# Engines' programs in the main sequence instead of a block, in a decode kernel on one core

## Chip, cores and metric

The kernel runs on one core of one Trainium2 chip. The metric is the device time of one execution in microseconds (us); lower is better. The time before is the median of three runs, 193.99 us (193.94 to 194.02).

A core has five engines, each with an instruction stream of its own: TensorE (PE, its weight loads PEld), VectorE (DVE), ScalarE (ACT), GpSimd (POOL) and SyncE (SP). They meet only through semaphores. SP, ACT and POOL can issue DMAs, which 16 DMA engines carry out.

## What is computed

One token of a decoder layer: normalised input, grouped-query attention against a cache of 16384 keys and values (32 query heads, 8 key/value heads, head size 128), an output projection and a residual; then a second normalisation and an MLP. The reference, cut to what matters (the data are bfloat16):

```python
def _A_ref(x, k_cache, v_cache, wq, wo):       # x [1,1,512], caches [1,8,16384,128]
    q = (x @ wq).reshape(B, Sq, 32, 128).transpose(0, 2, 1, 3)
    k = jnp.repeat(k_cache, 4, axis=1)
    v = jnp.repeat(v_cache, 4, axis=1)
    p = softmax(einsum("bhqd,bhkd->bhqk", q, k) * 128 ** -0.5)
    o = einsum("bhqk,bhkd->bhqd", p, v)
    return o.transpose(0, 2, 1, 3).reshape(B, Sq, 4096) @ wo

def _B_ref(x, w1, w2, w3, w4):                 # with one token hs is zero: w1, w2 drop out
    ...
    x1 = x + hs
    h2 = gelu(layernorm(x1) @ w3) @ w4         # w3 [512,1792], w4 [1792,512]
    return x1 + h2

h  = A_x + _A_ref(layernorm(A_x), A_k_cache, A_v_cache, A_wq, A_wo)
h2 = h + _B_ref(layernorm(h), B_w1, B_w2, B_w3, B_w4)
```

With a single token the four shifted quarters of the mixer are all padding, so hs is zero and the kernel doesn't load w1 and w2.

## The kernel before

The 79 MB of keys, values and weights are streamed through four buffers `rb` of 4 MB (`RING`, line 124), in the order of `ORDER` (line 125): wq, the keys of two heads, then values and keys in turn, at last wo and the MLP's weights. All these loads are issued by SP through `load` (line 216); only the small input x4 is issued by ACT (line 302). The loop of line 444 runs over the 8 key/value heads: DVE transposes a head's keys in eight pieces (line 379), PE multiplies them by the queries (line 387), a maximum over all scores is taken (lines 394 to 408), ACT applies the exponential (line 409), and PE multiplies the weights by the values of the head before (line 428). Behind the loop stand the output projection (line 494), the normalisation, the two MLP products (lines 507 and 528) and the last addition, which writes the tile `fin` on DVE (line 532). SP stores `fin` (line 534), a DMA of 4 rows of 256 bytes, and a no-operation on SP that is marked as reading `out` (line 536) makes SP wait until the store has landed.

How the code becomes instruction streams is what matters here. The class `Program` (line 24) collects operations: `op` (line 35) appends each to the list of its engine, `self.ops`, and notes which earlier operations it depends on. Nothing is written until `emit` (line 72). It numbers the operations that someone waits for and gives each engine a semaphore that counts them (lines 77 to 85). Then it opens a block (line 86) and, for each engine, hands the function that `_engine` returns (line 92) to the block's method for this engine (lines 87 to 89); the function goes through the engine's list and writes each operation's waits (line 102) and the operation itself (line 104). The block is entered through the `ExitStack` that the kernel opens at line 150, so that it is left where that `with` ends. For this reason the profile puts the instructions of the block's end under L150: a branch, a drain on each engine (it waits until what the engine has in flight is done) and a meeting of all engines over two semaphores, which GpSimd gathers and releases.

A meeting of the same kind stands at the program's start, ahead of the kernel's own instructions. It is written where the program object is made, and the profile has it under L553, with four small constants that GpSimd fills.

Of the kernel before, what the change touches and what calls it, by code (L numbers as in the profile page):

```python
# [23 lines left out]
class Program:  # L24
# [47 lines left out]
    def emit(self):  # L72
        for ops in self.ops.values():
            for o in ops:
                for d in o.deps:
                    d.needed = True
        for e, ops in self.ops.items():
            if not any(o.needed and o.dma is None for o in ops):
                continue
            sem = self.ctx.enter_context(self.nc.semaphore(f"e_{e}"))  # L80
            n = 0
            for o in ops:
                if o.dma is None and o.needed:
                    n += 1
                    o.sem, o.val = sem, n
        block = self.ctx.enter_context(self.nc.Block())
        for e, at in (("SP", block.sync), ("POOL", block.gpsimd), ("PE", block.tensor),
                      ("ACT", block.scalar), ("DVE", block.vector)):
            at(self._engine(self.ops[e]))

    @staticmethod
    def _engine(ops):
# [475 lines left out]
```

## Time and profile before

| | us |
|---|---|
| median of three runs | 193.99 (193.94 to 194.02) |
| profiled execution, its time | 193.82 |
| its span, first to last instruction | 191.7 |
| PE busy | 118.5 (62%) |
| DVE busy | 107.6 (56%) |
| ACT busy | 10.0 (5%) |
| POOL busy | 8.8 (5%) |
| DMA queue of the loads, share of 16 engines | 96.9% |
| read from memory | 79.17 MB, 413 GB/s over the span |
| mean granted TensorE clock | 0.87 |

A profile is one execution. Its span goes from the first to the last recorded instruction; the execution's time is a little longer, as something is done ahead of and behind the recorded instructions. The page gives the busy time of each engine over the span; instructions that only the engine's sequencer handles (semaphore instructions, branches, drains, the issue of a DMA) are not counted as busy, and an engine's name with a q (SPq, ACTq) stands for its sequencer. The chain of waits is followed back from the last instruction: at each step to whatever released it.

The page's strip of the busy share in 40 equal slices, in tenths (9 is 90% or more), shows how steady the stream of loads is and how the last slice differs:

```profile
DMA  6999999999999999999999999999999999999991
```

### The profile page before, as it was taken

The page shows a single profiled execution, that of the slowest core. Times are in us where ns is not written, and L with a number is a line of the kernel's source. Part 1 is how long each engine was busy: PE and PEld are TensorE (multiplying, and loading weights), DVE is VectorE, ACT ScalarE, POOL GpSimd, SP SyncE. Part 2 cuts the span into 40 slices and gives each one's busy share as a digit, 9 for nine tenths or more (in the row PEclk, how much of TensorE's full clock was granted, in tenths as well). Part 3 has the DMA queues.
Part 4 walks back from the last instruction along what each step waited for, and adds up shares of the span by engine and source line. Part 5 has one row for each costly group of instructions (what it writes and reads, how often), then busy time and mean ns, then how long its engine had stood idle before and what let it go on. Part 6 is the DMA issues. An engine that isn't in the chain of part 4 may idle for free.

```text
span 191.7 us, 2236 instructions
## 1 busy us (share of the span) xinstructions
PE 118.5 (62%) x962; PEld 53.1 (28%) x962; DVE 107.6 (56%) x178; ACT 10.0 (5%) x22; POOL 8.8 (5%) x19
## 2 busy tenths in 40 slices
PE   1025079479799825982499349953994399456343
PEld 1024024124243321432143213331332133214211
DVE  5822099498589318932793269426952595203260
ACT  3000000100100100010001000010001000400010
POOL 6400000000000000000000000000000000000060
PEclk9999999969969985999589966997999579969955
DMA  6999999999999999999999999999999999999991
GB/s 219 438 438 434 438 439 431 438 438 438 431 427 438 438 438 424 427 397 424 424 431 438 434 438 438 438 431 438 431 431 421 438 431 438 391 412 404 424 378 49
DMA packets 3912, 79.29 MB, mean 414 GB/s; under 512 B 448, under 2 KB 448, under 8 KB 1216
## 3 DMA queue, kind: packets, MB, share of 16 engines
q1 hardware_dynamic: 3896, 79.17, 96.9%
q8 instruction: 7, 0.11, 0.2%
q14 instruction: 1, 0.01, 0.0%
q10 hardware_dynamic: 8, 0.00, 0.0%
HBM read 79.17 MB, written 0.00 MB: 413 GB/s over the span
## 4 chain that ended last, share of the span: by engine, by line
DMA 66%; DVE 21%; PE 5%; SPq 5%; issue 1%; ACT 0%; ACTq 0%
DMA rb<-in_A_k_cache_dram 56%; DVE kt L379 20%; DMA rb<-in_B_w_dram 10%; SPq L217 5%; PE s_ps L387 5%; ACT p_sb L409 0%; DVE pt L414 0%; DVE mx L394 0%; PE mn_ps L528 0%; PE mn_ps L404 0%; PE mn_ps L398 0%; DVE nm L400 0%; DVE fin L532 0%; DVE nmh L406 0%; SPq L102 0%
## 5 line engine op out<-in xcount | busy, mean ns | idle before, releaser
L387 PE MATMUL s_ps<-kt,qb 128*128 128x512 bf16 x256 | 71.9, 442 | 34.8 <-DVE kt L379 34.3
L379 DVE STREAM_TRANSPOSE kt<-rb 128x1024 int32<-128x1024 int32 x64 | 73.0, 1207 | 30.1 <-DMA rb<-in_A_k_cache_dram 30.1
L387 PEld LDWEIGHTS s_ps<-kt,qb 128*128 128x128 bf16 x256 | 26.2, 109 | 77.9 <-DVE kt L379 44.3
L428 PE MATMUL O_ps<-rb,pt 128*16 128x512 bf16 x256 | 20.3, 404 | 3.7 <-DMA rb<-in_A_v_cache_dram 3.7
L439 PE MATMUL A_ps<-o_sb,zo 128*128 128x128 f32 x64 | 9.7, 296 | 7.4 <-DVE o_sb L436 7.4
L409 ACT ACTIVATE p_sb<-s_ps,bias 128x512 bf16<-128x512 f32 x8 | 5.5, 687 | 154.8 <-DVE nmh L406 154.8
L394 DVE TENSOR_REDUCE mx<-s_ps 128x1 f32<-128x512 f32 x8 | 5.5, 692 | 10.0 <-PE s_ps L387 10.0
L439 PEld LDWEIGHTS A_ps<-o_sb,zo 128*128 128x128 f32 x64 | 8.1, 197 | 8.5 <-DVE o_sb L436 8.5
L436 DVE COPY o_sb<-O_ps 128x512 f32<-128x512 f32 x8 | 5.3, 657 | 8.1 <-PE O_ps L428 8.1
L414 DVE STREAM_TRANSPOSE pt<-p_sb 128x512 bf16<-128x512 bf16 x8 | 5.7, 712 | 7.2 <-ACT p_sb L409 7.2
L358 PE MATMUL mn_ps<-xn,rb 128*128 128x1 bf16 x128 | 3.6, 165 | 9.3 <-DMA rb<-in_A_wq_dram 9.3
L428 PEld LDWEIGHTS O_ps<-rb,pt 128*16 128x16 bf16 x256 | 5.8, 91 | 10.4 <-DMA rb<-in_A_v_cache_dram 5.6
L292 POOL TENSOR_SCALAR st<-st 128x1 f32<-128x1 f32 x1 | 0.3, 264 | 175.6 <-DVE st L277 175.6
L358 PEld LDWEIGHTS mn_ps<-xn,rb 128*128 128x128 bf16 x128 | 3.5, 104 | 9.3 <-issue 9.3
L398 PE MATMUL mn_ps<-ident_f,mx 128*1 128x128 f32 x16 | 3.0, 270 | 2.5 <-DVE mx L394 2.5
L418 PE MATMUL A_ps<-acc,zd 128*128 128x1 f32 x16 | 3.1, 260 | 2.3 <-ACT p_sb L409 2.3
L400 DVE TENSOR_REDUCE nm<-mn_ps 1x4 f32<-1x128 f32 x8 | 2.2, 279 | 3.8 <-PE mn_ps L398 3.8
L343 POOL MEMSET qb<- 128x4992 bf16 x1 | 4.3, 4257 | 0.0
L494 PE MATMUL O_ps<-rb,o_b 128*32 128x128 bf16 x128 | 2.3, 220 | 2.7 <-DMA rb<-in_A_wo_dram 1.6
L418 PEld LDWEIGHTS A_ps<-acc,zd 128*128 128x128 f32 x16 | 2.4, 188 | 5.9 <-ACT p_sb L409 5.9
L362 DVE CAST QT<-mn_ps 128x32 bf16<-128x32 f32 x1 | 0.2, 193 | 6.0 <-PE mn_ps L358 6.0
L528 PE MATMUL mn_ps<-rb,hcol 128*32 128x128 bf16 x56 | 2.3, 307 | 2.0 <-DVE hcol L523 1.2
(72 smaller groups left out, 42.4 us busy)
## 6 DMA issues: line engine op xcount, KB each, us to landing
rb<-in_A_k_cache_dram SPq DMA_DIRECT2D x8, 4096.0 KB, 29.7
rb<-in_A_v_cache_dram SPq DMA_DIRECT2D x8, 4096.0 KB, 35.0
rb<-in_A_wq_dram SPq DMA_DIRECT2D x1, 4096.0 KB, 12.2
rb<-in_A_wo_dram SPq DMA_DIRECT2D x2, 1280.0 KB, 30.1
rb<-in_B_w_dram SPq DMA_DIRECT2D x1, 1344.0 KB, 23.5
rb<-in_A_wo_dram SPq DMA_DIRECT2D x1, 1024.0 KB, 32.4
rb<-in_B_w_dram SPq DMA_DIRECT2D x1, 640.0 KB, 25.3
rb<-in_A_wo_dram SPq DMA_DIRECT2D x1, 512.0 KB, 33.2
```

Of the source, the lines that this page charges most:

```text
L217: P.op(by, lambda e: e.dma_start(dst, src), w=[key, *also], dma=name)
L343: pool(lambda e: e.memset(qb[:, :, :, :], 0.0), w=["qb"])
L358: pe(lambda e, h=h, k=k: e.matmul(n_ps[:, h:h + 1], wq_sb[:, k * HQ * DH + h * DH:k * HQ * DH + (h + 1) * DH], xn[:, k:k + 1], start=(k == ...
L379: dve(lambda e, i=i, view=view: e.transpose(view(kt), view(rb[i])), r=[("r", i, n) for n in range(RPARTS)], w=[("kt", t)])
L387: pe(lambda e, g=g, n=n, c=c: e.matmul(s_ps[:, g % 2, :], qb[:, n, g, QPAD - 4 * c:QW - 4 * c], ktv[:, n // 2, n % 2, :, 8 * c:8 * c + 8, ...
L394: dve(lambda e, g=g: e.tensor_reduce(mx[:, :], s_ps[:, g % 2, :], AX.X, ALU.max), r=[("s", g % 2)], w=["mx"], bank=[("s", g % 2)])
L409: act(lambda e, g=g: e.activation(p_sb[:, :], s_ps[:, g % 2, :], ACTF.Exp, bias=bias[:, 0:1], scale=float(SCALE), accum_out=acc[g % 2][:, :]),
L414: dve(lambda e, g=g: e.transpose(pt[g % 2][:, :, :].rearrange("p n u -> p (n u)"), p_sb[:, :]), r=["p"], w=[("pt", g % 2)])
L418: pe(lambda e, g=g: e.matmul(A_ps[:, 128:129], zd[:, 112 - 16 * g:240 - 16 * g], acc[g % 2][:, :], start=(g == 0), stop=(g == HKV - 1), sk ...
L428: pe(lambda e, q=q, ct=ct, xl=xl, ch=ch: e.matmul(O_ps[g % 2][32 * ct:32 * ct + 16, :], pt[g % 2][:, xl, 4 * ch:4 * ch + 16], tiles[:, xl ...
L436: dve(lambda e, g=g: e.tensor_copy(o_sb[g % 2][:, :], O_ps[g % 2][:, :]), r=[("O", g % 2)], w=[("osb", g % 2)], bank=[("O", g % 2)])
L439: pe(lambda e, g=g, j=j: e.matmul(A_ps[:, 0:128], zo[:, j, 112 - 16 * g:240 - 16 * g], o_sb[g % 2][:, j * 128:(j + 1) * 128], start=False, ...
```

## The change

`emit` no longer opens a block. It calls the function of each engine with the engine object itself, so that the operations are written into the sequence the program is in already, the main one, behind its opening meeting. The engines are gone through in a slightly different order (ACT second instead of fourth). Everything else is as it was: the lists of operations, their semaphores and waits, the store and the no-operation on SP behind it.

```diff
@@ -83,10 +83,9 @@
                 if o.dma is None and o.needed:
                     n += 1
                     o.sem, o.val = sem, n
-        block = self.ctx.enter_context(self.nc.Block())
-        for e, at in (("SP", block.sync), ("POOL", block.gpsimd), ("PE", block.tensor),
-                      ("ACT", block.scalar), ("DVE", block.vector)):
-            at(self._engine(self.ops[e]))
+        for e, eng in (("SP", self.nc.sync), ("ACT", self.nc.scalar), ("POOL", self.nc.gpsimd),
+                       ("PE", self.nc.tensor), ("DVE", self.nc.vector)):
+            self._engine(self.ops[e])(eng)
 
     @staticmethod
     def _engine(ops):
```

## The prediction

> **What bounds the kernel now.** I read the chain of waits first, because only work on it can move the end. By its shares the kernel is a stream of loads: DMA 66%, then the key transposes on VectorE. The change touches none of that. So the second view is the chain in order of time, its last pieces:
>
> ```profile
> 169.27 19.55 DMA rb<-in_B_w_dram
> 188.82 0.04 issue
> 188.86 0.43 PE mn_ps L528 x6
> 189.30 0.02 issue
> 189.32 0.29 DVE fin L532
> ```
>
> The columns are start, length and what it was, in us. The reader is to see that the last piece of arithmetic ends at 189.32 + 0.29 = 189.61, while the span is 191.7: two microseconds lie behind it, and the change is there. The third view, the timeline of the last stretch, names the next step:
>
> ```profile
> 189.64 0.63 SPq L534 DMA_DIRECT2D out_dram<-fin  x1
> ```
>
> SyncE issues the store of the result at 189.64 and has issued it at 190.27. The fourth view is SyncE's own waits:
>
> ```profile
> SPq L150 <- DMA out_dram<-fin: 1.0, 1, 1.0
> SPq L553 <- PEq L553: 0.7, 1, 0.7
> SPq L150 <- PEq L150: 0.2, 1, 0.2
> ```
>
> SyncE waits 1.0 us for the store to land, and then 0.2 us more for a meeting of the engines. L150 is the line under which the block's end is recorded, L553 the program's opening meeting. The view of line 150 is the thing removed, all of it (count, shortest/median/longest in ns, first and last start in us):
>
> ```profile
> L150 POOLq EVENT_SEMAPHORE  x2: 17/17/17, 191.5 to 191.6; - x2
> L150 ACTq DRAIN  x1: 879/879/879, 185.1 to 185.1; - x1
> L150 POOLq DRAIN  x1: 564/564/564, 186.4 to 186.4; - x1
> L150 PEldq DRAIN  x1: 450/450/450, 188.9 to 188.9; - x1
> L150 DVEq DRAIN  x1: 326/326/326, 189.3 to 189.3; - x1
> L150 SPq COMPARE_BRANCH  x1: 33/33/33, 191.3 to 191.3; - x1
> L150 SPq DRAIN  x1: 7/7/7, 191.4 to 191.4; - x1
> L150 SPq EVENT_SEMAPHORE  x1: 17/17/17, 191.6 to 191.6; - x1
> L150 ACTq EVENT_SEMAPHORE  x1: 17/17/17, 191.6 to 191.6; - x1
> L150 DVEq EVENT_SEMAPHORE  x1: 21/21/21, 191.6 to 191.6; - x1
> L150 PEldq EVENT_SEMAPHORE  x1: 51/51/51, 191.6 to 191.6; - x1
> ```
>
> Four engines have drained by 189.7; everything else of the meeting hangs on SyncE's branch, which carries the wait on the store. The view rounds starts to 0.1 us; the same records in nanoseconds, with the store's last increment ahead of them, are
>
> ```
> 191277         store's semaphore reaches its value
> 191293 .. 191326  SyncE  COMPARE_BRANCH
> 191449 .. 191456  SyncE  DRAIN
> 191482 .. 191499  GpSimd EVENT_SEMAPHORE (gather)
> 191559 .. 191576  GpSimd EVENT_SEMAPHORE (release)
> 191601 .. 191618  SyncE  EVENT_SEMAPHORE
> 191614 .. 191665  TensorE EVENT_SEMAPHORE, end of the span
> ```
>
> **The change part by part.** The profiled execution took 193.82 us and its span is 191.665, so 2.155 us lie around the span and no row shows them. The median of the runs shown is 193.99; I work out a difference on the profiled execution and take it off the median.
>
> Removed from the path: from the branch's start to the last release, 191.665 - 191.293 = 0.372 us. It is made of the branch (0.033), what lies between a taken branch and the next instruction (0.123), SyncE's drain (0.007), the step to GpSimd (0.026), its two semaphore instructions and the gap between them (0.094), the step to TensorE (0.038) and TensorE's semaphore instruction (0.051).
>
> Left in its place: SyncE still waits on the store, now on the no-operation of L536 or on a semaphore instruction, with nothing behind it. The trace of before has neither at this place: the wait had moved onto the branch. The nearest rows are SyncE's semaphore instruction, 0.017, and the branch without its jump, 0.033. I take 0.02. So 0.372 - 0.02 = 0.35 us off the span, which should end near 191.31.
>
> Removed off the path: the drains of ScalarE (0.879), GpSimd (0.564), TensorE (0.450) and VectorE (0.326). The last ends at 189.661, 1.6 us before the store lands at 191.277; the flight of the store hides them, worth 0. Without that cover only 0.05 us would show, from the end of fin (189.610) to the end of VectorE's drain.
>
> The entry: the opening meeting releases SyncE at 0.654 and its first load starts at 0.722; a branch would have to stand between, and none is recorded on any engine. SyncE's usual step from a semaphore instruction to a load is 159.743 to 159.773, 0.030, so at most 0.068 - 0.030 = 0.04 could come off, and it would count in full, since the first load heads the DMA stream. I take 0. The new order of the five calls (ScalarE ahead of GpSimd) changes no engine's own sequence; neither do loops, semaphores and waits: 0. No DMA moves past another on any queue, as each engine's list of operations is written out as before.
>
> What lies behind the span is the uncertain term. Today all five engines leave within 0.047 us of each other (191.618 to 191.665); afterwards four leave between 186 and 189.7 and SyncE at 191.31. If the end of the launch only follows the last engine, its 2.155 us stay. If it collects engines one after the other, four of five steps may be done before SyncE comes; the nearest row for one step is GpSimd's release reaching SyncE and passing it, 191.618 - 191.576 = 0.042, so 4 x 0.042 = 0.17 at most. In the other direction, if something in the closing takes its time from the last computing instruction and not from SyncE, the meeting was hidden beside it and up to the whole 0.35 is given back. As the row nearest to such a closing is the meeting itself, in which one hub serves all at nearly the same time, I take less than half of the upper bound, 0.07.
>
> The Trainium skill ("Runtime: NRT & Kernel Launch", "The ~15µs preamble/postamble breakdown") speaks partly against the change: the runtime brings a barrier of its own behind every kernel, so the kernel's own meeting was a second one, and one remains. It states the meeting as a chain of eight hops of 44 ns; by the page four hops may be passed early and the sum would be 0.35 + 0.18 = 0.53, an estimate. No record here reaches past the span.
>
> The sum: 0.35 + 0 + 0 + 0.07 = 0.42 us, 193.99 - 0.42 = 193.57 (for the profiled execution 193.82 - 0.42 = 193.40).
>
> **The rivals.** (a) Nothing comes of it: what follows the span is not gated by SyncE's end but by something the 0.37 us ran beside. For it: the profiled time has 2.155 us that no row explains. Against it: in the records everything after 190.3 hangs on SyncE alone. Time 193.99 - 0.35 + 0.35 = 193.99; with half given back 193.82.
>
> (b) A larger gain: four engines do closing work of their own, slower on GpSimd or TensorE than on SyncE, and now do it under the store. The nearest rows are the opening, where GpSimd is busy from 0.135 to its release at 0.612, 0.48 us, and SyncE itself runs 7 ns of drain. Price 0.35 + 0.48 = 0.83, time 193.16. Against it: GpSimd's opening is memsets that a closing need not have.
>
> (c) Slower: ScalarE (last work ends 185.956) and GpSimd (186.884) go into their closing code while the last pieces of w4 still land (188.819), and fetch it through the same 16 DMA engines. The rows: instruction packets of 8 KB took 0.309 to 0.455 us. Two on the same DMA engine, one of the sixteen that the last piece needs, hold it up by 0.62 to 0.91; less 0.42 that is 0.20 to 0.49 later, some 0.35, 194.34. It decides from a delay of 0.42 on. Against it: the DMA engines' mean busy share is 0.27 from 187.3 to 188.8, the last 1.5 us before that landing, and an 8 KB instruction packet at 28.1 us shows code being fetched long before an engine's program is through.
>
> (d) The change doesn't do what it says: the wait at L536 has no branch to ride on and is lost, SyncE ends at 190.27. Then 191.665 - 190.27 = 1.40 come off, 192.59. For it: L536 left no record before. Against it: the wait did survive, moved onto the branch, so it is not thrown away.
>
> **How the numbers follow.** The forecast as I have it, a gain between 0.29 (the whole path with 0.06 given back) and 0.55 (0.35 + 0.17, and 0.03 for the scatter of the runs), 193.44 to 193.70, gets 0.62; (a) 0.14, (b) 0.13, (c) 0.06, (d) 0.05. What a measurement of this kernel can tell from no change is about 0.2%, 0.39 us, that is 193.60: the forecast lies almost on it. Of its 0.62 I count 0.40 below and 0.22 above. Faster: 0.40 + 0.13 + 0.05 = 0.58. Same: 0.22 + 0.14 = 0.36. Slower: 0.06. The range goes from (b)'s price, 193.15, to where about a third of (a) is left out, 193.95; outside stay (c), (d) and parts of (a) and (b), some 0.2.
>
> **What would show it.** In the profile of the changed kernel: no record under the block's end on any engine, the span near 191.3 with SyncE's wait on the store as its last record (190.27 if neither wait nor no-operation is recorded), about 2224 instructions (2236 less the twelve of the view), the first load still near 0.72, and a landing of the last w4 piece still 0.50 us before fin starts (189.321 - 188.819). A run time that falls by more than the span shows the term behind the span. The forecast is wrong if the time falls by less than 0.25 us (something else gates the end), by more than 0.6 us (closing work was on the path), or if the last w4 landing moves later by 0.3 us or more with instruction packets beside it (rival c).

## The result, and the profile after

| | before | after |
|---|---|---|
| median | 193.96 us (193.79 to 194.02, 6 runs) | 192.98 us (192.76 to 193.05, 6 runs) |
| ratio | | 0.995, 95% interval 0.9939 to 0.996 |
| profiled execution: its time | 193.82 | 192.76 |
| its span | 191.665 | 191.216 |
| time around the span | 2.155 | 1.544 |
| the store's landing to the end of the execution | 2.543 | 1.577 |

The changed kernel is 0.98 us faster; the interval makes that 0.8 to 1.2 us. More than half of it lies around the span, where the views list no instruction. Behind the block's last lines nothing is left: the views of the lines around the opened `with` are empty, and SyncE's own waits of the changed kernel (engine and line, what it waited for, total us, times, longest) end with the store:

```profile
SPq L533 <- DVE fin L531: 17.7, 1, 17.7
...
SPq L535 <- DMA out_dram<-fin: 1.0, 1, 1.0
SPq L552 <- PEq L552: 0.7, 1, 0.7
```

(Lines are one lower than before, as the change is one line shorter.) The third line of the view of before, the 0.2 us of waiting for TensorE under the block's end, is gone. What took the place of the branch is seen in the view of line 535:

```profile
L535 SPq EVENT_SEMAPHORE  x1: 17/17/17, 191.2 to 191.2; - x1
```

The wait on the store is a semaphore instruction of 17 ns, and it is the last instruction recorded. Ahead of it, the last pieces of the chain of waits of the changed kernel are those of before:

```profile
169.15 19.57 DMA rb<-in_B_w_dram
188.73 0.04 issue
188.77 0.43 PE mn_ps L527 x7
189.20 0.02 issue
189.23 0.29 DVE fin L531
```

From the matrix products on, each comes 0.09 us sooner than before, all for one reason: the last piece of w4 landed at 188.726 and not at 188.819. That is scatter of the stream of loads, which the change doesn't touch; the spans of the changed kernel's six runs lie between 191.2 and 191.5.

So the two profiled executions are better compared from the store's landing on, and there the 0.966 us (2.543 - 1.577) fall into two parts. From the landing to the end of the last instruction it was 191.665 - 191.277 = 0.388 and is 191.216 - 191.183 = 0.033: 0.355 us, the meeting. Around the span it was 2.155 and is 1.544: 0.611 us, with no instruction in the views.

### The profile page after: what moved, and what is told of

Read it like the earlier page. It is cut to its first block, busy times and chain, and to the rows that moved or that the text cites. A ratio compares the mean times of both kernels' runs of the same rounds, so it can differ in the third digit from the quotient of the medians.

```text
span 191.2 us, 2225 instructions
## 1 busy us (share of the span) xinstructions
PE 120.5 (63%) x962; PEld 54.7 (29%) x962; DVE 107.5 (56%) x178; ACT 10.0 (5%) x22; POOL 8.8 (5%) x19
## 4 chain that ended last, share of the span: by engine, by line
DMA 67%; DVE 25%; SPq 5%; PE 1%; issue 1%; ACT 0%; ACTq 0%
DMA rb<-in_A_k_cache_dram 56%; DVE kt L378 24%; DMA rb<-in_B_w_dram 10%; SPq L216 5%; PE s_ps L386 1%; ACT p_sb L408 0%; DVE pt L413 0%; DVE mx L393 0%; PE mn_ps L527 0%; PE mn_ps L403 0%; PE mn_ps L397 0%; DVE nm L399 0%; DVE fin L531 0%; DVE nmh L405 0%; SPq L101 0%
## 5 line engine op out<-in xcount | busy, mean ns | idle before, releaser
L386 PEld LDWEIGHTS s_ps<-kt,qb 128*128 128x128 bf16 x256 | 25.7, 108 | 78.3 <-DVE kt L378 45.8
L438 PE MATMUL A_ps<-o_sb,zo 128*128 128x128 f32 x64 | 10.2, 307 | 7.4 <-DVE o_sb L435 7.4
L438 PEld LDWEIGHTS A_ps<-o_sb,zo 128*128 128x128 f32 x64 | 8.6, 208 | 8.9 <-DVE o_sb L435 8.9
L493 PE MATMUL O_ps<-rb,o_b 128*32 128x128 bf16 x128 | 3.6, 312 | 1.0 <-DVE o_b L487 1.0
L493 PEld LDWEIGHTS O_ps<-rb,o_b 128*32 128x32 bf16 x128 | 3.3, 145 | 1.2 <-DVE o_b L487 1.2
```

The costliest lines, as they stand in the source:

```text
L386: pe(lambda e, g=g, n=n, c=c: e.matmul(s_ps[:, g % 2, :], qb[:, n, g, QPAD - 4 * c:QW - 4 * c], ktv[:, n // 2, n % 2, :, 8 * c:8 * c + 8, ...
L438: pe(lambda e, g=g, j=j: e.matmul(A_ps[:, 0:128], zo[:, j, 112 - 16 * g:240 - 16 * g], o_sb[g % 2][:, j * 128:(j + 1) * 128], start=False, ...
L493: pe(lambda e, r_=r_, q=q: e.matmul(O_ps[0][32 * q:32 * q + 32, 0:128], copies(o_b[:, r_:r_ + 1], 32), wo_sb[:, r_ * D + q * 128:r_ * D + ...
```

## Experiments

All spans are so alike in their opening (the first load starts 0.72 us into the span in each profile) that I read the time around the span as a measure of what follows the last instruction. It repeats to some hundredths in each kernel, though the spans of single runs are on record to 0.1 us only: 2.12 to 2.23 in all runs of the kernel before, 1.50 to 1.59 in those of the changed one.

Theory "closing": each engine has closing work behind its last instruction, of a length of its own; the meeting let all five start it only after the store, and the changed kernel lets four do it early. The rivals are named with each run.

**The meeting alone, without block and branch** (e1). Behind the changed kernel a meeting of all engines is written into the main sequence.

```diff
         P.emit()
+        nc.all_engine_barrier()
```

> The changed kernel with a meeting of all engines (a drain on each, gathered and released by GpSimd) written behind it in the main sequence: the meeting is back, the block and SyncE's branch are not. The changed kernel stood 0.98 us under the one before, some 0.4 of it in the span and 0.6 behind it. Theory 'closing' (each engine has closing work of its own behind its last instruction, longer on some engine than on SyncE, and the meeting kept it from starting early): the 0.6 behind the span comes back, and 0.23 of the span; about 0.15 us under before, which is the branch and its jump. Theory 'chain' (the launch's end collects the engines one after the other, the early ones for nothing): the same, about -0.15. Theory 'branch' (the taken branch of SyncE makes its closing code come late): only the meeting's 0.22 come back, about -0.76.

Measured: 193.82 us against 193.83, ratio 0.9998 (0.9989 to 1.0007), and 2.17 us around the span, as before. The view of the added line shows the meeting of the kernel before once more, without the branch:

```profile
L537 POOLq EVENT_SEMAPHORE  x2: 17/17/17, 191.6 to 191.7; - x2
...
L537 SPq DRAIN  x1: 7/7/7, 191.6 to 191.6; - x1
L537 SPq EVENT_SEMAPHORE  x1: 17/17/17, 191.8 to 191.8; - x1
...
L537 PEldq EVENT_SEMAPHORE  x1: 51/51/51, 191.8 to 191.8; - x1
```

The meeting brings the whole gain back. Theory "branch" (-0.76) is out; the -0.15 of the other two lies inside the interval, which goes from -0.21 to +0.14 us.

**The jump alone** (e7). The kernel before, block and meeting kept; the no-operation counts up a semaphore, so that it stays an instruction and carries the wait itself.

```diff
-        P.op("SP", lambda e: e.nop(), r=["out"])
+        P.op("SP", lambda e: e.nop(), r=["out"]).needed = True
```

> The kernel before with one thing changed: SyncE's last no-operation adds one to a semaphore, so that the wait for the store stays on an instruction of its own and SyncE has no recorded branch at the block's end; block and meeting stay. Theory 'closing': only the jump goes, 0.10 to 0.12 of the span, the 2.17 around it stays: about 0.1 us under before. Theory 'branch': the 0.6 around the span goes with the jump, about 0.75 under before.

Measured: 193.78 against 193.81, ratio 0.9995 (0.9986 to 1.0004), 2.19 around the span. The records show what the jump is worth: from the start of SyncE's wait instruction to the last release it is 0.372 us before, 0.311 here and 0.270 in e1. A gain of 0.06 to 0.10 us is inside both intervals, and so is none. The 0.6 are not the jump's: without it the time around the span is still 2.19.

**All engines late, no meeting** (e2). Each engine gets its own wait for the store.

```diff
         P.op("SP", lambda e: e.nop(), r=["out"])
+        P.op("ACT", lambda e: e.nop(), r=["out"])
+        P.op("POOL", lambda e: e.nop(), r=["out"])
+        P.op("PE", lambda e: e.nop(), r=["out"])
+        P.op("DVE", lambda e: e.nop(), r=["out"])
```

> The changed kernel with a wait for the store at the end of ScalarE, GpSimd, TensorE and VectorE too, each on its own: all five engines leave together, as behind the meeting, but without meeting, drain or branch. Theory 'closing': the 0.6 us behind the span come back, so about 0.38 us under before. Theory 'chain': the same. Theory 'branch': nothing comes back, 0.98 under before.

Measured: 193.48 against 193.83, ratio 0.9979 (0.997 to 0.9988), 2.16 around the span. The views of the five lines show engines that know nothing of each other and leave within 0.05 us (SyncE at 191.521, TensorE at 191.567):

```profile
L535 SPq EVENT_SEMAPHORE  x1: 17/17/17, 191.5 to 191.5; - x1
...
L536 ACTq EVENT_SEMAPHORE  x1: 17/17/17, 191.5 to 191.5; - x1
...
L537 POOLq EVENT_SEMAPHORE  x1: 17/17/17, 191.5 to 191.5; - x1
...
L538 PEldq EVENT_SEMAPHORE  x1: 51/51/51, 191.5 to 191.5; - x1
...
L539 DVEq EVENT_SEMAPHORE  x1: 21/21/21, 191.5 to 191.5; - x1
```

The 0.6 us around the span are back, the meeting's 0.3 are not. They belong to the four engines being late, not to the meeting's instructions. Theory "branch", which wanted nothing back, is out here too.

**One engine late beside SyncE** (e3 to e6). The same with a single added line, for GpSimd, TensorE, ScalarE and VectorE in turn; e3 reads

```diff
         P.op("SP", lambda e: e.nop(), r=["out"])
+        P.op("POOL", lambda e: e.nop(), r=["out"])
```

GpSimd:

> The changed kernel with a wait for the store at the end of GpSimd alone, beside SyncE's. Theory 'closing': if GpSimd has the long closing, the whole 0.6 comes back (0.38 under before), else nothing (0.98 under). Theory 'chain': at most a part of it, as the other three are still early: -0.98 to -0.8. Theory 'branch': -0.98.

TensorE:

> The changed kernel with a wait for the store at the end of TensorE alone, beside SyncE's. Theory 'closing': if TensorE has the long closing, the whole 0.6 comes back (0.38 under before), else nothing (0.98 under). Theory 'chain': at most a part of it: -0.98 to -0.8. Theory 'branch': -0.98.

ScalarE:

> The changed kernel with a wait for the store at the end of ScalarE alone, beside SyncE's. So far the time around the span is 1.55 us with SyncE alone late, 1.82 with TensorE late too, 2.08 with GpSimd, 2.16 with all. Theory 'closing' (the time behind the span is that of the late engine with the longest closing): the 2.16 of all five needs an engine that has it, ScalarE or VectorE; if it is ScalarE this run shows 2.16 and stands 0.35 us under before, if not anything between 1.55 and 2.16. Theory 'sum' (each late engine adds its part): 0.27 and 0.53 are already more than the 0.61 of all, so ScalarE must add nothing: 1.55, 0.98 under before. Theory 'chain' (a late engine costs the steps that come after its place): a value on the same scale as TensorE's and GpSimd's, 1.55 to 2.16.

VectorE:

> The changed kernel with a wait for the store at the end of VectorE alone, beside SyncE's. Theory 'closing': 2.16 around the span (0.35 us under before) if VectorE has the longest closing, else between 1.55 and 2.16; at least one of VectorE and ScalarE has to show 2.1 or more. Theory 'sum': 1.55. Theory 'chain': a value between 1.55 and 2.16 that, with the others, makes steps of similar size.

Measured, beside the kernel before of the same chip, with the mean of the time around the span:

| late | us | before | ratio (95%) | around the span |
|---|---|---|---|---|
| SyncE alone (the changed kernel) | 192.98 | 193.96 | 0.995 (0.9939 to 0.996) | 1.55 |
| with ScalarE | 192.98 | 193.81 | 0.996 (0.9948 to 0.9973) | 1.68 |
| with VectorE | 193.01 | 193.81 | 0.9962 (0.9948 to 0.9975) | 1.75 |
| with TensorE | 193.24 | 193.83 | 0.9966 (0.9953 to 0.9978) | 1.81 |
| with GpSimd | 193.38 | 193.83 | 0.9976 (0.9966 to 0.9986) | 2.08 |
| all five | 193.48 | 193.83 | 0.9979 (0.997 to 0.9988) | 2.16 |

How such a row is read, with GpSimd's: the view of its added line and the span of the same profile are

```profile
L536 POOLq EVENT_SEMAPHORE  x1: 17/17/17, 191.1 to 191.1; - x1
```

```profile
core 0: 191.1 us, clock 0.854
```

GpSimd's instruction is the last record, it ends 8 ns after SyncE's, and yet the execution's time is 193.22: 2.09 us later, where the changed kernel, with SyncE's as its last, needs 1.54. Each engine has a value of its own. Theory "sum" fell: it wanted 1.55 for ScalarE and VectorE, and the four additions to 1.55 would make 1.55 + 0.13 + 0.20 + 0.26 + 0.53 = 2.67 of all five. Theory "closing" as I had it for e5 and e6 fell in one point: neither ScalarE nor VectorE has the 2.16 of all five; GpSimd's 2.08 is the largest. Its price for TensorE, all of the 0.6 us or nothing, missed as well: 0.26 came back. Theory "chain" missed with its prices for e3 and e4, at most 0.18 back for either: it was 0.53 and 0.26.

**SyncE not late** (e8, e9). The wait is moved: SyncE ends with the issue of the store, ScalarE or GpSimd waits for it. For e8:

```diff
-        P.op("SP", lambda e: e.nop(), r=["out"])
+        P.op("ACT", lambda e: e.nop(), r=["out"])
```

> The changed kernel with the wait for the store moved from SyncE to ScalarE: SyncE ends with the issue of the store, ScalarE alone is late. From the store's landing to the end of the execution the profiled runs took 1.58 us (SyncE alone late), 1.74 (with ScalarE too), 1.78 (VectorE), 1.89 (TensorE), 2.13 (GpSimd), 2.23 (all), 2.54 before. Theory 'closing', by which the longest closing among the late engines counts and nothing else: ScalarE's own is 1.74, so 1.74 here and about 0.83 us under before. Theory 'crowd' (engines that close at the same time hold each other up, which would explain that all five take 0.1 more than GpSimd): less than 1.74, towards 1.58, about 0.98 under before or better.

> The changed kernel with the wait for the store moved from SyncE to GpSimd. Theory 'closing': GpSimd's 2.13 from the landing to the end stays whether SyncE is late too or not, about 0.45 us under before. Theory 'crowd': less than 2.13 by what SyncE beside it cost.

Measured: ScalarE 193.13 against 193.86, ratio 0.9957 (0.9945 to 0.997), from the landing to the end 1.739 (late beside SyncE it was 1.740). GpSimd 193.43, ratio 0.9976 (0.9967 to 0.9985), 2.130 (beside SyncE 2.132). Whether SyncE is late or long done makes no difference, to 0.002 us in the profiled runs; "crowd" is out for these two pairs. And neither of the two is better suited than SyncE to wait for the store: ScalarE takes 0.16 us more, GpSimd 0.55. TensorE and VectorE were not tried without SyncE. None of these runs beats the changed kernel.

**Several late** (e10, e11). GpSimd and TensorE beside SyncE; then ScalarE, VectorE and TensorE beside SyncE, with GpSimd early.

```diff
+        P.op("POOL", lambda e: e.nop(), r=["out"])
+        P.op("PE", lambda e: e.nop(), r=["out"])
```

> The changed kernel with GpSimd and TensorE late beside SyncE. Theory 'closing': the longer of 2.13 and 1.89 from the landing to the end, 2.13, about 0.45 us under before. Theory 'crowd': more, up to the 2.23 of all five, about 0.35 under before. If each added its own part it would be 1.58 + 0.55 + 0.32 = 2.45.

> The changed kernel with ScalarE, VectorE and TensorE late beside SyncE, GpSimd early. Theory 'closing': TensorE's 1.89 from the landing to the end, about 0.6 us under before. Theory 'crowd': more than 1.89, about 2.0, some 0.5 under before. If the 2.23 of all five didn't come from GpSimd: 2.23.

Measured: e10 193.38 against 193.86, ratio 0.9975 (0.9965 to 0.9986), 2.109 from the landing to the end; e11 193.33, ratio 0.9974 (0.9965 to 0.9984), 2.025. In e10 the longer counts, GpSimd's 2.13, and TensorE's 1.89 is hidden beneath it. In e11 the longest of the three alone is TensorE's 1.893, and together they take 0.13 more. So the longest is most of it, and something of about 0.1 us comes on top when ScalarE, VectorE and TensorE are late together, in e11 as in e2 (2.233 against GpSimd's 2.132). Where it stands is seen at the end of this section.

**Late, but not too late** (e12). ScalarE, GpSimd and TensorE get a last wait as in e2, but for VectorE's `fin` instead of the store.

```diff
+        P.op("ACT", lambda e: e.nop(), r=["fin"])
+        P.op("POOL", lambda e: e.nop(), r=["fin"])
+        P.op("PE", lambda e: e.nop(), r=["fin"])
```

> The changed kernel with a last wait on ScalarE, GpSimd and TensorE, as in the late kernels, but for fin, VectorE's last tile (done near 189.5 us), and not for the store (landed near 191.2). It tells lateness from the mere added instruction. Theory 'closing': GpSimd needs 2.07 us from its last instruction to the end and has 192.98 - 189.5 = 3.4; nothing is lost, 1.55 around the span and 0.98 us under before. If the added wait itself or its place at an engine's end costs the time: GpSimd's 0.5 comes back, about 0.45 under before.

Measured: 192.82 against 193.80, ratio 0.9952 (0.9939 to 0.9966), 1.56 around the span. GpSimd's added instruction is in the view of its line, 1.6 us ahead of the end of the span:

```profile
L537 POOLq EVENT_SEMAPHORE  x1: 17/17/17, 189.6 to 189.6; - x1
```

The added waits cost nothing as long as the engine is through in time. It is lateness that costs.

**What follows the last instruction** (no new run; the traces of the runs above). The traces also hold the increments of the semaphores, and these go on behind the last instruction, where the views list nothing. Semaphore 2, which no instruction of the kernel uses, is counted up nine times there, and nine times more 0.8 us later. The first nine, in ns from the span's start, with the end of the last instruction of the engine named:

```
late               1      2      3      4      5      6      7      8      9   its end
SyncE alone   189394 189428 189467 189662 191333 191376 191414 191448 191496   191216
with ScalarE  189340 191297 191335 191380 191403 191500 191540 191574 191620   191188
with VectorE  189351 189385 189424 191361 191384 191482 191521 191555 191602   191214
with TensorE  191588 191622 191660 191704 191727 191825 191864 191898 191945   191396
with GpSimd   189276 189310 191666 191710 191734 191831 191870 191904 191951   191129
before        191904 191938 192149 192194 192217 192314 192354 192388 192434   191576 (GpSimd)
```

The trace doesn't say who counts, but each late engine holds up one increment, always the same: the first comes after TensorE's end, the second after ScalarE's, the third after GpSimd's, the fourth after VectorE's, the fifth after SyncE's. So the five engines are collected in a fixed order, and four more increments close the round. Where no engine holds it up on the way, as with TensorE, the round takes 0.357 us, in steps of 0.023 to 0.098. And each engine has a way of its own from its last instruction to its increment: 0.109 us on ScalarE, 0.117 on SyncE, 0.147 on VectorE, 0.192 on TensorE, but 0.537 on GpSimd (the same in e2, e3, e9, e10 and e12; 0.573 in the kernel before). "Chain" and "closing" were each half of it: the time after the landing is set by whichever engine's own way, and the steps that follow its place, end last.

The landing, the ninth increment and the end of the execution split every profile in two:

| late | landing to the ninth increment, us | from there to the end, us |
|---|---|---|
| SyncE alone | 0.313 | 1.264 |
| with ScalarE | 0.470 | 1.270 |
| with VectorE | 0.435 | 1.348 |
| with TensorE | 0.628 | 1.265 |
| with GpSimd | 0.863 | 1.269 |
| with GpSimd and TensorE | 0.863 | 1.246 |
| with ScalarE, VectorE and TensorE | 0.658 | 1.367 |
| all five | 0.864 | 1.369 |
| before | 1.157 | 1.386 |

The first column is the round just described. The second is 1.25 to 1.27 in the eight profiles where VectorE is early and 1.35 to 1.43 in the six where it is late (e1 and e7 among them). So the 0.1 us that e11 and e2 had on top goes with VectorE, not with the number of late engines. What it is stays open: in the second round the sixth increment comes 0.47 us after the fifth in before, e1 and e7 and 0.10 in all others, so it doesn't explain e2, e6 and e11, and the reported end moves by less than that. Ahead of the span the last round of semaphore 2 begins 0.37 us before the first instruction in every profile, so the difference doesn't lie there.

## Why the prediction was wrong

The direction was right, the time was not: 192.98 against 193.57 and a range that ended at 193.15.

**The path that is removed: right.** The span was to lose 0.35 us from the landing on, and lost 0.355. A wait of 0.02 was to stay in place of the 0.372, and it is a semaphore instruction of 0.017. 2224 instructions were foretold and there are 2225; the one is that wait. The drains' cover held, the first load starts at 0.720, and nothing of the entry changed.

**The term behind the span: wrong, and the whole of the miss.** I took 0.07 us, "less than half of the upper bound", out of a bound of 4 x 0.042 = 0.17, one step of a semaphore for each of four engines that come early. Measured: 0.611 in the profiled executions, 0.63 in the mean of the runs (2.18 against 1.55). The sum with it would have been 0.355 + 0.61 = 0.97; the medians gave 0.98.

The step that failed is the bound. The picture behind it, "if it collects engines one after the other, four of five steps may be done before SyncE comes", is what the increments show, and the steps that came off the path are worth 0.122 us: from GpSimd's increment to the ninth it was 0.285 before, from SyncE's it is 0.163 now. That is inside the 0.17. But the prediction let every engine enter the collection as soon as its last instruction was over, and put the way from there to its increment at nothing. On GpSimd it is 0.573 us, on SyncE 0.117. GpSimd's increment came 0.484 us behind the end of the span, SyncE's comes 0.117 behind it now: 0.367 us less. The remaining 0.122 lie behind the ninth increment (1.386 against 1.264) and go with VectorE being late; they had no term either. 0.122 + 0.367 + 0.122 = 0.611.

Two readings led there. "All five engines leave within 0.047 us of each other" leaves out GpSimd, whose last record ends at 191.576, 0.089 before the end of the span, and it was GpSimd that the others then waited for. And "no record here reaches past the span" holds for instructions only: the trace of before has increments up to 193.954, and its third one comes 0.211 us after the second, where the second round has 0.038 at this place. One engine was waited for, and that could be seen.

**Rival (b) named what was left out.** "Four engines do closing work of their own, slower on GpSimd or TensorE than on SyncE" fits the ways measured: GpSimd's is 0.42 us longer than SyncE's (0.537 against 0.117). TensorE's is only 0.08 longer; that it costs 0.32 in all is mostly due to its place at the head of the order, with 0.357 us of steps behind it against SyncE's 0.163. Its price of 0.48, from GpSimd's opening, lay between that 0.42 and the 0.61 of the whole term: close by luck, as no run ties the opening to the way to an increment. I gave it 0.13, because the opening is memsets that a closing need not have, and let the range end at its price instead of beyond it. 2.155 us without an instruction were in sight, and a term of that size should have had the wider bound.

**The Trainium skill on it.** The page ("Runtime: NRT & Kernel Launch", "The ~15µs preamble/postamble breakdown") gives the eight hops of 44 ns, some 355 ns, for the meeting ahead of the kernel. The increments behind the kernel agree with it: eight steps, 0.357 us, when TensorE is late. The estimate of 0.18 for four hops was of the right size for the steps alone (0.122); like mine it left out an engine's way to its increment. That a barrier remains behind the kernel agrees with the nine increments on a semaphore that the kernel doesn't use.

**The other rivals.** (a), nothing comes of it, and (d), the lost wait, are refuted by time and by the record of the wait. (c), instruction packets beside the last loads, did not come (its price was low: the seven packets of q8 inside the span of before are of 16 KB and took 0.99 to 1.10 us each, not 0.31 to 0.46). The page of the changed kernel lists the same packets as that of before,

```profile
q8 instruction: 7, 0.11, 0.2%
q14 instruction: 1, 0.01, 0.0%
```

and the last of w4 landed 0.50 us before `fin` started, as before.

**What is shown and what is not.** Shown: the meeting costs 0.3 us in its own records (e2 against before, 2.54 - 2.23 from the landing to the end) and 0.66 by making the other engines late; which engine is late sets the amount, by its way to its increment and its place in the order; an engine may be late for nothing as long as SyncE's path ends after its own. Not shown: what GpSimd does in its 0.54 us, and what the 0.1 us behind the ninth increment is that goes with VectorE. The split into steps and ways is from one profile of each kernel; the times of the runs bear it out for each engine (0.13, 0.20, 0.26 and 0.53 us over SyncE).

## What to carry to other kernels

A meeting of all engines at the end of a kernel cost twice here: its own records, and the way out of the slowest engine, which could have run under the last store. Let each engine's program end as early as its work allows, and let only SyncE stay for the store, as it had the shortest way out here (1.55 us against GpSimd's 2.08): it is collected last of the five, and its own way is 0.12 us. A meeting that ends on GpSimd puts the longest way behind the store. Where a kernel's time is longer than its span, the difference is a term like any other: compare it from run to run, look for semaphore increments in it, and price a change to what comes last with all of it as the bound.

## What the runs showed of the hardware

The time around the span is no constant of the launch. It depends on which engines are last, from 1.55 us (SyncE) over 1.68 (ScalarE), 1.75 (VectorE) and 1.81 (TensorE) to 2.08 (GpSimd), and it repeats to some hundredths from chip to chip (2.12 to 2.23 for the kernel before on four of them). Behind the last instruction the five engines are collected one after the other, TensorE, ScalarE, GpSimd, VectorE, SyncE, over one semaphore, in 0.357 us when none is waited for; GpSimd's increment comes 0.54 us after its last instruction, those of the others 0.11 to 0.19. The jump over a block's end, which looked like 0.12 us in the records, gave 0.06 to 0.10 from the wait to the last release when it was taken away.
